# Moving the softmax denominators' small operations in the first two batches, and clearing less of a buffer

## The chip, the cores and the metric

The kernel runs on one core of a Trainium2 chip. The metric is the device time of one execution in microseconds (us), median of several runs. The kernel before takes 1670.19 us (three runs, 1670.05 to 1670.26). Five engines work beside each other, each through its own queue of instructions: TensorE (PE in the profile; PEld is its weight load), VectorE (DVE), ScalarE (ACT), GpSimd (POOL) and SyncE (SP), which issues most of the DMA transfers. All arithmetic is in fp32.

## The reference

Eight batches of eight heads, 576 positions, 64 values per head. Attention drops scores more than `tau` below the row's maximum; a Fourier mixing and a two-layer network follow:

```
scores = (q @ k.T) / 8
scores = where(scores >= max(scores) - tau, scores, -1e9)
attn   = exp(scores - max(scores))
attn   = attn / (sum(attn) + 1e-9)
x      = attn @ v                      # heads side by side: (8, 576, 512)
u      = x + real(fft(fft(x, axis=1), axis=2))
un     = (u - mean(u)) / sqrt(var(u) + 1e-6)
out    = u + relu(un @ w_ch1) @ w_ch2
```

The change concerns `sum(attn) + 1e-9`, its inverse, and where the inverse meets the product with `v`.

## The kernel before

**Steps.** Heads are taken in pairs, four pairs to a batch. A pair has five steps: four of 128 query rows of both heads, and one (`t == 4`) of the last 64 rows of both heads in one tile. So a batch has 20 steps (`per_batch`), numbered `i` over all batches.

**Softmax of a step** (`softmax`, from L450). TensorE puts the scores of the two heads in two PSUM tiles `sc` (L433; L444 in the fifth step). VectorE takes the negated maxima (L461), ScalarE the exponentials `e` (L469) and the threshold `thr` (L473). VectorE then masks `e` and sums it into `den` in one instruction per head (L477), adds 1e-9 (L482, one per head) and takes the reciprocal of both (L489). The scores' tiles are free for the next step when both L477 are done.

**Two ways to divide.** From the third batch on (`normalized`), VectorE and ScalarE multiply `e` by the reciprocal (L492, L496). In the first two batches GpSimd instead spreads the reciprocals over 64 columns per head (`rec`, L501); TensorE transposes this next to the weights, ScalarE copies it to `recs`, and VectorE multiplies by `recs` as it takes the product with `v` out of PSUM (L597).

**Transposed weights of a step** (`weights_in_parts`, L512, called whole by `transposed_weights`). It follows one step behind: after the softmax of step `i` has been issued, step `i - 1` is transposed. TensorE transposes the last 64 keys of both heads (`e[:, 512:640]`, L541) and `rec` (L544) into the tile `pe`, then the other keys (L560) into `pw`. ScalarE copies `pe` to `ends` and `recs` (L548, L552), and `pw` to `e_t` (L562, L564). `weighted_values` (L569) multiplies `v` with `e_t` and lastly `ends` (`pv`, L589).

**Beside it in the first two batches** the network's weights come in. They arrive as 64-bit floats and are converted in chunks of 128x512 (`convert`, L281) by every engine in turn: VectorE takes mantissa and exponent bits (L298, L301), ScalarE turns them into floats (L306, L309, L312), VectorE adds the low word (L314), and GpSimd multiplies by exponent and sign (L319, L320). The first batch converts 16 chunks of `w_ch1`, one in a step. The second batch converts 16 chunks of `w_ch2` by a table (`PLAN`, L1271), in some steps two, while TensorE already runs the Fourier mixing and the network's first groups (L822, L848).

**Order.** Up to the end of the second batch the order on every engine is the program's order (`by_hand`, closed at L1384). In `step` (first batch) and `second_batch` it is: scores, softmax of step `i` with the last stages of the previous chunk between maxima and exponentials, the filler or mixing work, the next chunk's first stages, `transposed_weights(i - 1)`, and more work. In the first batch the first stages of a chunk (L298, L301) come ahead of `transposed_weights`; in the second batch they are issued by `transfers`, `advance` and the calls around it, mostly behind it. After the second batch only TensorE's order is fixed by hand, and a planner orders the other engines.

**The folds' buffer.** `f` (L93, four chunks of two halves of `FW` = 304 columns) first holds the rows of a Fourier table for `copy_seq` (L221), and is then cleared whole by GpSimd (L230). Later `fold_rows` (L611) writes folded rows of `x` into it: in each half columns 0 to 142, 143 or 144 in one half, 160, and 161 to 303. The columns in the gap are read by `fold_halves` and by the mixing's matmuls, so they must be zero.

Of the kernel before, what the change touches and what calls it, by code (L numbers as in the profile page):

```python
# [9 lines left out]
FP32 = mybir.dt.float32  # L10
INT32 = mybir.dt.int32
UINT32 = mybir.dt.uint32
ALU = mybir.AluOpType
# [15 lines left out]
def _repeated(ap, n):  # L29

    return bass.AP(
        tensor=ap.tensor,
        offset=ap.offset,
        ap=[list(ap.ap[0]), list(ap.ap[1]), [0, n]],
    )
# [12 lines left out]
def kernel(  # L48
# [12 lines left out]
    nc = tc.nc  # L61
    B, H, S, D = q.shape
# [4 lines left out]
    NT = 5  # L67
# [17 lines left out]
    ps = ctx.enter_context(tc.tile_pool(name="ps", bufs=2, space=bass.MemoryType.PSUM))  # L85
# [7 lines left out]
    f = const.tile([128, ND, 2 * FW], FP32, name="f")  # L93
# [71 lines left out]
    ident = const.tile([128, 128], FP32, name="ident")  # L165
# [5 lines left out]
    for u in range(2):  # L171
# [10 lines left out]
        out=q_scale[:], in0=tau_t[:], scalar1=0.0, scalar2=SCALE, op0=ALU.is_ge, op1=ALU.mult  # L182
# [3 lines left out]
        out=below[:], in0=tau_t[:], scalar1=0.0, scalar2=-3.0e38, op0=ALU.is_lt, op1=ALU.mult  # L186
# [3 lines left out]
        out=tau_pos[:], in0=tau_t[:], scalar1=0.0, scalar2=-1.0, op0=ALU.max, op1=ALU.mult  # L190
# [30 lines left out]
    def copy_seq():  # L221
        nc.gpsimd.memset(seq_xe[:, :, :], 0.0)
        nc.gpsimd.memset(seq_xo[:, :, :], 0.0)
        for u, (pieces, dst, parity, parts) in enumerate(SEQ):
            for p, n in parts:
                for c in range(2):
                    nc.gpsimd.tensor_copy(
                        dst[p : p + n, c, :], f[p : p + n, u, KH * c + parity : KH * (c + 1) : 2]
                    )
        nc.gpsimd.memset(f[:, :, :], 0.0)  # L230

# [145 lines left out]

    heads = {}  # L380
    steps = {}
    xs = {}
    sums = {}

# [33 lines left out]
    def normalized(n):  # L418


        return n >= 2 * NPAIR
# [28 lines left out]
    def softmax(i, between=None, meanwhile=None):  # L450

        t = i % NT
        sc, nh = steps[i]
        neg = sb.tile([128, 2], FP32, tag="neg", bufs=3, name="neg")
        thr = sb.tile([128, 2], FP32, tag="thr", bufs=3, name="thr")
        den = sb.tile([128, 2], FP32, tag="den", bufs=3, name="den")


        e = sb.tile([128, 2 * S], FP32, tag="e", name="e")
        for j in range(nh):  # L460
            nc.vector.tensor_reduce(  # L461
                out=neg[:, j : j + 1], in_=sc[j][:, :, 0:HALF], axis=AXIS_XY, op=ALU.max,
                negate=True,
            )
        if meanwhile is not None:
            meanwhile()
        for j in range(nh):
            ej = e[:, S * j : S * (j + 1)].rearrange("p (c n) -> p c n", c=2)
            nc.scalar.activation(  # L469
                out=ej, in_=sc[j][:, :, 0:HALF], func=ACT.Exp, bias=neg[:, j : j + 1], scale=1.0  # L470
            )
            if j == 0:
                nc.scalar.activation(  # L473
                    out=thr[:, 0:nh], in_=neg[:, 0:nh], func=ACT.Identity,
                    bias=thr_off[:, :], scale=-1.0,
                )
            nc.vector.scalar_tensor_tensor(  # L477
                out=ej, in0=sc[j][:, :, 0:HALF], scalar=thr[:, j : j + 1], in1=ej,
                op0=ALU.is_ge, op1=ALU.mult, accum_out=den[:, j : j + 1],
            )  # L480

            nc.vector.tensor_scalar(  # L482
                out=den[:, j : j + 1], in0=den[:, j : j + 1], scalar1=1e-9, scalar2=None,
                op0=ALU.add,
            )
            if between is not None:
                between()
                between = None
        nc.vector.reciprocal(den[:, 0:nh], den[:, 0:nh])  # L489
        rec = None  # L490
        if normalized(i // NT):
            nc.vector.tensor_scalar(  # L492
                out=e[:, 0:S], in0=e[:, 0:S], scalar1=den[:, 0:1], scalar2=None, op0=ALU.mult
            )
            if nh == 2:
                nc.scalar.activation(  # L496
                    out=e[:, S : 2 * S], in_=e[:, S : 2 * S], func=ACT.Copy, scale=den[:, 1:2]
                )
        else:
            rec = sb.tile([128, 2 * D], FP32, tag="rec", name="rec")  # L500
            nc.gpsimd.tensor_copy(  # L501
                rec[:, :].rearrange("p (j d) -> p j d", j=nh), _repeated(den[:, 0:nh], 2 * D // nh)
            )
        if t == 4:
            nc.scalar.copy(e[:, S : S + 64], e[:, 512:S])
        steps[i] = (e, rec)

    def transposed_weights(i):
        for _ in weights_in_parts(i):
            pass  # L510

    def weights_in_parts(i):  # L512

        n, t = divmod(i, NT)
        e, rec = steps.pop(i)
        if t in (0, 2):

            e_t = sb.tile([128, 8, S - 256], FP32, tag="e_t", bufs=1, name="e_t")  # L520
            ends = sb.tile([128, S - 256], FP32, tag="ends", bufs=1, name="ends")
            recs = None
            if rec is not None:
                recs = sb.tile([128, S - 256], FP32, tag="sums", bufs=1, name="recs")
            vt = heads[n][2]
            if t == 0 and PAIRS[n % NPAIR] % 2:

                vt = sb.tile([128, 10, D], FP32, tag="vr", bufs=1, name="v_rev")
                src = heads[n][2]
                nc.gpsimd.tensor_copy(vt[:, :, 0:1], src[:, :, 0:1])  # L530
                last = src[:, :, D - 1 : D]
                down = bass.AP(
                    tensor=last.tensor, offset=last.offset,
                    ap=[list(last.ap[0]), list(last.ap[1]), [-1, D - 1]],
                )
                nc.gpsimd.tensor_copy(vt[:, :, 1:D], down)
            heads[n] = (*heads[n][0:2], vt, e_t, ends, recs)
        e_t, ends, recs = heads[n][3:6]
        q0 = 128 * (t - (0 if t < 2 else 2))
        pe = ps.tile([128, 4, 128], FP32, tag="mm", bufs=4, name="pe")  # L540
        nc.tensor.transpose(pe[:, 0, :], e[:, 512:640], ident[:, :])  # L541
        kept = [ends]
        if rec is not None:
            nc.tensor.transpose(pe[:, 1, :], rec[:, :], ident[:, :])  # L544
            kept.append(recs)
        for c, dst in enumerate(kept):
            if t < 4:
                nc.scalar.copy(dst[:, q0 : q0 + 128], pe[:, c, :])  # L548
            else:
                for j in range(2):  # L550
                    hp = slice(64 * j, 64 * j + 64)
                    nc.scalar.copy(dst[hp, q0 : q0 + 64], pe[hp, c, hp])  # L552
        qs = slice(q0, q0 + (128 if t < 4 else 64))
        for j in range(2 if t < 4 else 1):
            pw = ps.tile([128, 4, 128], FP32, tag="mm", bufs=4, name="pw")
            if j == 1:
                yield
            for c in range(4):
                c0 = (S + D) * j + 128 * c
                nc.tensor.transpose(pw[:, c, :], e[:, c0 : c0 + 128], ident[:, :])  # L560
            if t < 4:
                nc.scalar.copy(e_t[:, 4 * j : 4 * j + 4, qs], pw[:, :, :])  # L562
            else:
                nc.scalar.copy(  # L564
                    e_t[:, :, qs].rearrange("p (j c) q -> p j c q", j=2),
                    pw[:, :, :].rearrange("p c (j q) -> p j c q", j=2),
                )

    def weighted_values(n, part):  # L569

# [614 lines left out]
    def step(i):  # L1185
# [9 lines left out]
        if t == 1 and n > 0:  # L1195
            softmax(i, lambda: weighted_values(n - 1, 1), last_stages)
            load_v(n + 1)
        elif t == 3:
            softmax(i, lambda: weighted_values(n, 0), last_stages)
        else:  # L1200
            softmax(i, None, last_stages)
# [56 lines left out]
    load_v(1)  # L1258
    copy_dim(raw)
    copy_seq()  # L1260
    LAST = HID // WC - 1
    for g in range(LAST):
# [124 lines left out]
    for i in range(2 * per_batch, total + 1):  # L1387
# [4 lines left out]
        n, t = divmod(i, NT)  # L1392
        if t > 2:
            fold_more()
        nothing = iter(())
        prep = prep_in_parts(n + 1) if t == 3 and n + 1 < B * NPAIR else nothing
        weights = weights_in_parts(i - 1)
        next(prep, None)
        fill()
# [71 lines left out]
```

## Time and profile before

| engine | busy, us | share of the span | instructions |
|---|---|---|---|
| TensorE (PE) | 1621.8 | 97% | 10826 |
| VectorE (DVE) | 1146.0 | 69% | 2518 |
| ScalarE (ACT) | 837.9 | 50% | 1817 |
| GpSimd (POOL) | 581.9 | 35% | 779 |

The span of the profiled execution is 1669.6 us. The first two batches' steps fill the time up to about 290 us. The instructions of which the change speaks, with their durations over the whole run:

| line | engine, operation | count | median, ns |
|---|---|---|---|
| L482 | DVE, add 1e-9, 128x1 | 288 | 153 |
| L489 | DVE, reciprocal, 128x2 or 128x1 | 160 | 166 |
| L477 | DVE, mask and sum, 128x576 | 288 | 810 |
| L501 | POOL, copy to `rec`, 128x128 | 40 | 438 |
| L230 | POOL, memset of `f`, 128x2432 | 1 | 2292 |
| L298 / L301 | DVE, bits of a chunk, 128x512 | 32 / 32 | 568 and 642 in the two larger groups / 510 and 513 |
| L319 / L320 | POOL, two multiplications of a chunk | 32 / 32 | 1273 / 1293 in the larger groups |

A line of the timeline gives the start in us from the beginning of the span, the duration in us, the engine, the line, the operation, the output and inputs by the program's names, and in brackets how long the engine had been idle and what ended that.

### The profile page before, as it was taken

How to read it: one execution, taken by the hardware profiler on the slowest of the kernel's cores; microseconds unless marked ns; L12 is line 12 of the kernel's file. 1: busy time of each engine (PE TensorE's matmuls, PEld its weight loads, DVE VectorE, ACT ScalarE, POOL GpSimd, SP SyncE). 2: the span in 40 equal slices, each digit the busy share in tenths (PEclk: the TensorE clock that was granted, in tenths of full speed). 3: DMA queues.
4: the chain of work that ended last, by engine and by line, in shares of the span. 5: the costliest groups of instructions: out<-in, count | busy, mean ns of one | idle time of the engine just before them, and what ended most of it. 6: DMA issues, size and time to landing. Idle time of an engine off the chain costs nothing.

```text
span 1669.6 us, 28885 instructions
## 1 busy us (share of the span) xinstructions
PE 1621.8 (97%) x10826; PEld 1273.6 (76%) x10826; DVE 1146.0 (69%) x2518; ACT 837.9 (50%) x1817; POOL 581.9 (35%) x779
## 2 busy tenths in 40 slices
PE   8998899999999999999999999999999999999998
PEld 4555555577887888878888778887878788889998
DVE  6887785567757686857566858686677768664454
ACT  5775675544455454545354546454646455532111
POOL 5674562041321442134332143213242244215232
PEclk9999999999999999999999999999999999999999
DMA  5423222100010101000101010111001010000000
GB/s 157 121 55 110 73 73 56 30 20 21 19 39 15 29 15 42 23 28 8 28 22 35 10 34 15 42 22 29 22 16 42 22 32 4 14 1 13 14 13 13
DMA packets 130384, 57.48 MB, mean 34 GB/s; under 512 B 121123, under 2 KB 121125, under 8 KB 130246
## 3 DMA queue, kind: packets, MB, share of 16 engines
q1 hardware_dynamic: 128854, 55.35, 12.3%
q8 instruction: 86, 1.41, 0.4%
q14 instruction: 52, 0.43, 0.1%
q10 hardware_dynamic: 1392, 0.30, 0.1%
HBM read 46.02 MB, written 9.44 MB: 33 GB/s over the span
## 4 chain that ended last, share of the span: by engine, by line
PE 76%; DVE 15%; ACT 7%; issue 2%; POOL 1%; DVEq 0%; ACTq 0%; POOLq 0%
PE ph L926 23%; PE po L1090 18%; PE pv L589 8%; PE sc L433 7%; PE pw L560 5%; PE po L848 3%; DVE e L477 3%; DVE neg L461 2%; ACT e L469 2%; DVE hs L1051 2%; PE sc L444 2%; PE ph L822 1%; PE py L692 1%; PE pa L709 1%; PE pn L782 1%
## 5 line engine op out<-in xcount | busy, mean ns | idle before, releaser
L469 ACT ACTIVATE e<-sc,neg 128x576 f32<-128x576 f32 x288 | 212.6, 738 | 238.1 <-DVE neg L461 237.4
L461 DVE TENSOR_REDUCE neg<-sc 128x1 f32<-128x576 f32 x288 | 206.2, 750 | 171.4 <-PE sc L433 158.5
L477 DVE SCALAR_TENSOR_TENSOR e<-sc,thr,e 128x576 f32<-128x576 f32 x288 | 229.7, 811 | 57.5 <-ACT thr L473 54.2
L1090 PE MATMUL po<-w,hs 128*128 128x256 f32 x1024 | 246.3, 383 | 0.5 <-DVE u L804 0.5
L1090 PEld LDWEIGHTS po<-w,hs 128*128 128x128 f32 x1024 | 186.0, 190 | 33.6 <-issue 11.2
L926 PE MATMUL ph<-u_t,w 128*128 128x128 f32 x1536 | 187.2, 276 | 0.0
L926 PEld LDWEIGHTS ph<-u_t,w 128*128 128x128 f32 x1536 | 178.7, 192 | 4.4 <-issue 3.3
L560 PE MATMUL pw<-ident,e 128*128 128x128 f32 x1152 | 169.5, 274 | 10.4 <-ACT kT L406 2.7
L562 ACT COPY e_t<-pw 128x512 f32<-128x512 f32 x256 | 148.9, 596 | 59.8 <-PE pw L560 59.3
L433 PE MATMUL sc<-kT,qT 64*128 64x288 f32 x1024 | 168.6, 429 | 6.8 <-DVE e L477 6.0
L560 PEld LDWEIGHTS pw<-ident,e 128*128 128x128 f32 x1152 | 134.2, 141 | 29.3 <-issue 4.3
L935 DVE TENSOR_TENSOR hs<-ph,hs 128x512 f32<-128x512 f32 x160 | 106.9, 685 | 71.4 <-PE ph L926 46.8
L433 PEld LDWEIGHTS sc<-kT,qT 64*128 64x128 f32 x1024 | 93.2, 186 | 69.3 <-issue 37.2
L926 PE MATMUL ph<-t_u,s_w 128*128 128x128 f32 x1024 | 126.0, 276 | 2.2 <-POOL t_u L900 1.8
L804 DVE SCALAR_TENSOR_TENSOR u<-po,rstd,u 128x256 f32<-128x256 f32 (+1 forms) x164 | 75.4, 484 | 73.8 <-PE po L1090 71.9
L926 PEld LDWEIGHTS ph<-t_u,s_w 128*128 128x128 f32 x1024 | 119.4, 192 | 5.3 <-issue 2.6
L1090 PE MATMUL po<-hs,s_tile 128*128 128x256 f32 x512 | 122.1, 382 | 0.0
L496 ACT ACTIVATE e<-e,den 128x576 f32<-128x576 f32 x96 | 75.0, 781 | 67.4 <-DVE den L489 66.7
L1090 PEld LDWEIGHTS po<-hs,s_tile 128*128 128x128 f32 x512 | 93.6, 190 | 13.6 <-issue 2.1
L943 ACT ACTIVATE hs<-hs 128x512 f32<-128x512 f32 x112 | 69.4, 631 | 63.9 <-DVE hs L935 63.9
L622 POOL TENSOR_TENSOR half<-x 128x287 f32<-128x287 f32 x48 | 40.4, 862 | 125.5 <-ACT x L595 70.7
L1086 POOL TENSOR_TENSOR hs<-hs,s_tile 128x512 f32<-128x512 f32 x32 | 42.3, 1323 | 117.5 <-PE po L1090 113.8
(199 smaller groups left out, 2905.8 us busy)
## 6 DMA issues: line engine op xcount, KB each, us to landing
hs<-in_moe_w_ch_dram SPq DMA_DIRECT2D x23, 512.0 KB, 4.4
out_dram<-u SPq DMA_DIRECT2D x36, 256.0 KB, 2.2
qk_in<-in_q_dram SPq DMA_DIRECT2D x64, 128.0 KB, 2.3
v_in<-in_v_dram SPq DMA_DIRECT2D x64, 128.0 KB, 2.4
qk_in<-in_k_dram SPq DMA_DIRECT2D x31, 128.0 KB, 2.5
w<-in_moe_w_ch_dram SPq DMA_DIRECT2D x6, 512.0 KB, 8.4
qk_in<-in_k_dram SPq DMA_DIRECT2D x31, 64.0 KB, 2.3
stage<-in_moe_w_ch_dram SPq DMA_DIRECT2D x3, 512.0 KB, 3.8
```

The lines of the kernel that those rows point to most:

```text
L433: nc.tensor.matmul(sc[j][:, c, 0:HALF], qT[hp, 128 * t : 128 * t + 128], kT[hp, HALF * c : HALF * (c + 1)], start=True, stop=True,)
L461: nc.vector.tensor_reduce(out=neg[:, j : j + 1], in_=sc[j][:, :, 0:HALF], axis=AXIS_XY, op=ALU.max, negate=True,)
L469: nc.scalar.activation(out=ej, in_=sc[j][:, :, 0:HALF], func=ACT.Exp, bias=neg[:, j : j + 1], scale=1.0)
L477: nc.vector.scalar_tensor_tensor(out=ej, in0=sc[j][:, :, 0:HALF], scalar=thr[:, j : j + 1], in1=ej, op0=ALU.is_ge, op1=ALU.mult, accum_out ...
L496: nc.scalar.activation(out=e[:, S : 2 * S], in_=e[:, S : 2 * S], func=ACT.Copy, scale=den[:, 1:2])
L560: nc.tensor.transpose(pw[:, c, :], e[:, c0 : c0 + 128], ident[:, :])
L562: nc.scalar.copy(e_t[:, 4 * j : 4 * j + 4, qs], pw[:, :, :])
L589: nc.tensor.matmul(pv[64 * j : 64 * j + 64, 0:m], vt[:, 2 * c + j, :], e_t[:, 4 * j + c, 0:m] if c < 4 else ends[:, 0:m], start=(c == 0), ...
L804: nc.vector.scalar_tensor_tensor(out=u, in0=product, scalar=self.rstd[:, t : t + 1], in1=u, op0=ALU.mult, op1=ALU.add,)
L926: nc.tensor.matmul(banks[name][:, 128 * q : 128 * q + 128], left[c][:, 512 * part + 128 * q : 512 * part + 128 * q + 128], right[c], start ...
L935: nc.vector.tensor_tensor(out=to, in0=bank, in1=to if other is None else other, op=ALU.add)
L1090: nc.tensor.matmul(bank[:, 0 : DM // 2], left[p], right[p], start=start and p == 0, stop=p == NK - 1, skip_group_check=True,)
```

## The change

In the first two batches the 1e-9 leaves VectorE: one GpSimd instruction for both heads follows the softmax. The reciprocal (VectorE) and the copy to `rec` (GpSimd) become a closure in a list, `inverses`, which is emptied behind the next step's maxima, and also at the head of `weights_in_parts`. There the transposes of `e[:, 512:640]` and `rec` go behind the others. The aim is that VectorE has fewer small instructions between the masking and the work that follows. The clearing of `f` shrinks to the columns from 143 to 159 of each half, so that GpSimd is done sooner in the first step. The batches from the third on keep their form.

```diff
-        nc.gpsimd.memset(f[:, :, :], 0.0)
+        halves = f[:, :, :].rearrange("p d (c n) -> p d c n", c=2)
+        nc.gpsimd.memset(halves[:, :, :, S // 4 - 1 : 160], 0.0)
...
+        while inverses:
+            inverses.pop(0)()
         if meanwhile is not None:
             meanwhile()
...
-            nc.vector.tensor_scalar(
-                out=den[:, j : j + 1], in0=den[:, j : j + 1], scalar1=1e-9, scalar2=None,
-                op0=ALU.add,
-            )
+            if normalized(i // NT):
+                nc.vector.tensor_scalar(
+                    out=den[:, j : j + 1], in0=den[:, j : j + 1], scalar1=1e-9, scalar2=None,
+                    op0=ALU.add,
+                )
...
-        nc.vector.reciprocal(den[:, 0:nh], den[:, 0:nh])
         rec = None
         if normalized(i // NT):
+            nc.vector.reciprocal(den[:, 0:nh], den[:, 0:nh])
...
         else:
             rec = sb.tile([128, 2 * D], FP32, tag="rec", name="rec")
-            nc.gpsimd.tensor_copy(
-                rec[:, :].rearrange("p (j d) -> p j d", j=nh), _repeated(den[:, 0:nh], 2 * D // nh)
-            )
+            nc.gpsimd.tensor_scalar(
+                out=den[:, 0:nh], in0=den[:, 0:nh], scalar1=1e-9, scalar2=None, op0=ALU.add
+            )
+            def inverse():
+                nc.vector.reciprocal(den[:, 0:nh], den[:, 0:nh])
+                nc.gpsimd.tensor_copy(
+                    rec[:, :].rearrange("p (j d) -> p j d", j=nh),
+                    _repeated(den[:, 0:nh], 2 * D // nh),
+                )
+            inverses.append(inverse)
...
     def weights_in_parts(i):
+        while inverses:
+            inverses.pop(0)()
...
-        pe = ps.tile([128, 4, 128], FP32, tag="mm", bufs=4, name="pe")
-        nc.tensor.transpose(pe[:, 0, :], e[:, 512:640], ident[:, :])
...
+        def last_keys():
+            pe = ps.tile([128, 4, 128], FP32, tag="mm", bufs=4, name="pe")
+            nc.tensor.transpose(pe[:, 0, :], e[:, 512:640], ident[:, :])
...
+        if rec is None:
+            last_keys()
         qs = slice(q0, q0 + (128 if t < 4 else 64))
...
+        if rec is not None:
+            last_keys()
```

More of the change, by code (lines that the diff above doesn't have):

```diff
@@ L381 @@
     steps = {}
+    inverses = []
     xs = {}
@@ L539, in weights_in_parts @@
         q0 = 128 * (t - (0 if t < 2 else 2))
-        pe = ps.tile([128, 4, 128], FP32, tag="mm", bufs=4, name="pe")
-        nc.tensor.transpose(pe[:, 0, :], e[:, 512:640], ident[:, :])
[L542 to L552, printed above, removed]
+        def last_keys():
+            pe = ps.tile([128, 4, 128], FP32, tag="mm", bufs=4, name="pe")
+            nc.tensor.transpose(pe[:, 0, :], e[:, 512:640], ident[:, :])
+            kept = [ends]
+            if rec is not None:
+                nc.tensor.transpose(pe[:, 1, :], rec[:, :], ident[:, :])
+                kept.append(recs)
+            for c, dst in enumerate(kept):
+                if t < 4:
+                    nc.scalar.copy(dst[:, q0 : q0 + 128], pe[:, c, :])
+                else:
+                    for j in range(2):
+                        hp = slice(64 * j, 64 * j + 64)
+                        nc.scalar.copy(dst[hp, q0 : q0 + 64], pe[hp, c, hp])
+        if rec is None:
+            last_keys()
         qs = slice(q0, q0 + (128 if t < 4 else 64))
@@ L567, in weights_in_parts @@
                 )
+        if rec is not None:
+            last_keys()
     def weighted_values(n, part):
```

## The prediction

> **What bounds the kernel now.** I read the page first. TensorE is busy 97% of the span, yet the change lives only in the first two batches, so I asked for busy time by stretch.
>
> ```profile
> 0.00:100.00 100.00, 92.61 (x452) 51.36 (x453) 78.24 (x191) 67.81 (x147) 64.64 (x116) 0.98 0.46 130
> 100.00:200.00 100.00, 88.86 (x507) 55.04 (x506) 77.82 (x173) 60.83 (x145) 52.76 (x62) 0.98 0.27 77
> 200.00:300.00 100.00, 93.90 (x505) 56.12 (x504) 71.70 (x174) 62.06 (x143) 45.93 (x63) 0.98 0.24 66
> 300.00:400.00 100.00, 99.01 (x564) 63.79 (x563) 63.74 (x146) 48.71 (x108) 18.77 (x29) 1.00 0.10 26
> ```
>
> (Columns: stretch and length, then busy PE, PEld, DVE, ACT, POOL.) From 264 us on the chain of waits is nearly all TensorE. Before that it alternates between VectorE, ScalarE and TensorE. So what the first 264 us win or lose arrives whole at the end; nothing later can absorb it. Next, the timeline of VectorE and GpSimd in the first step and in one step of batch 1 (the second batch):
>
> ```profile
> 16.40 0.15 DVE L482 TENSOR_SCALAR den<-den 128x1 f32<-128x1 f32 x1
> 16.58 0.17 DVE L489 RECIPROCAL den<-den 128x2 f32<-128x2 f32 x1
> ...
> 16.86 2.29 POOL L230 MEMSET f<- 128x2432 f32 x1
> 17.01 2.42 DVE L301 TENSOR_SCALAR hs<-hs 128x512 int32<-128x512 int32 x1
> ...
> 25.09 0.20 POOL L530 COPY v_rev<-v_in 128x10 f32<-128x10 f32 x1 [0.52 <-DMA v_in<-in_v_dram]
> ...
> 71.00 0.42 DVE L298 TENSOR_SCALAR w<-hs 128x512 int32<-128x512 int32 x1
> ```
>
> ```profile
> 192.97 1.58 POOL L319 TENSOR_TENSOR w<-w,u_t 128x512 f32<-128x512 f32 x1 [7.33 <-DVE w L314]
> 194.63 1.29 POOL L320 TENSOR_TENSOR w<-w,w 128x512 f32<-128x512 f32 x1
> 195.88 1.46 POOL L319 TENSOR_TENSOR w<-w,u_t 128x512 f32<-128x512 f32 x1
> 197.42 1.36 POOL L320 TENSOR_TENSOR w<-w,w 128x512 f32<-128x512 f32 x1
> 198.73 0.29 POOL L501 COPY rec<-den 128x128 f32<-128x128 f32 x1
> ```
>
> ```profile
> 195.31 0.17 DVE L489 RECIPROCAL den<-den 128x2 f32<-128x2 f32 x1
> 195.39 0.81 DVE L298 TENSOR_SCALAR w<-w 128x512 int32<-128x512 int32 x1
> 196.13 1.50 DVE L301 TENSOR_SCALAR u_t<-w 128x512 int32<-128x512 int32 x1
> 197.55 1.41 DVE L461 TENSOR_REDUCE neg<-sc 128x1 f32<-128x576 f32 x2
> ```
>
> Two things are to be seen. L298 and L301 take 0.42 us alone and up to 1.5 us (2.42 under the memset) while GpSimd works. And in the step at 193 us GpSimd still multiplies weights until 198.8, 3.7 us after the last masking (L477) ended at 195.1.
>
> [...]L301 and the memset end within 0.3 us of each other, while the maxima L461 take 736 to 767 ns everywhere. [...]each engine's rows follow its program order. So a reciprocal that waits for GpSimd holds everything behind it on VectorE.
>
> **The change, part by part.**
>
> *Where the inverse goes.* The pending inverses are emitted behind the next maxima, but also at the head of the function that transposes weights. That function is called for step i-1 just after the softmax of step i has queued its inverse, so step i's reciprocal is emitted there. The order of the built instructions shows it: in batch 0 behind L298 and L301 of its own step, ahead of the next maxima; in batch 1 mostly straight behind L477, ahead of L298 and L301. Only steps 0 and 19 fall behind maxima. GpSimd's 1e-9 stands behind the L319/L320 pairs of that step.
>
> *Memset.* 2432 elements in a partition become 136. At 2.29 us for the whole I take 0.25 (the 288-element memset took 0.35; bounds 0.15 and 0.35). L301 then ends near 17.4 instead of 19.4, 1.9 us earlier. But L530 waits for a DMA until 25.09, and L319 stands behind it, so GpSimd's pair gains only some 1.0 us by then. I count **-1.0** (bounds -1.9 and -0.5).
>
> *Additions off VectorE (72 of them, 40 steps of two or one).* L482 lasts 153 ns. The chain before holds 25 pieces of it (3.9 us) and 11 of L489 (1.7 us). Most of this isn't won, for two reasons. In batch 0 a conversion step is a loop: L314 ends, 0.14, the two multiplies 2.65, L298 ends 0.25 after them, L301 0.43, maxima 1.33, L314 0.67: 5.47 us, against 5.42 and 5.43 between L314 at 20.7, 26.1 and 31.5. [...]In the other steps only the second L477 moves, by 0.11 us (its start after the first one's end). The page of waits gives 16 score matmuls waiting for L477; at about 8 of them the 0.11 counts: **-0.9**.
>
> *Reciprocal in batch 0.* It takes 0.17 us behind L301, but the copy to rec (0.28 to 0.57) no longer slows L301 (0.51 instead of 0.42). Even: **0**. The copy to rec now waits about 1 us more on GpSimd. That is hidden where GpSimd idles 1 to 4 us before L319, but not between 95.9 and 110.7, where it never idles (L377, the folds L627, L651, L652, and the pairs). Two such waits cost 0.4 to 0.8[...]: **+1.0**.
>
> *Addition on GpSimd.* No row shows it. A 128x2 operation there (L632) takes 0.20; I take 0.25 with 0.1 for each handover, bounds 0.15 and 0.5. Where GpSimd is idle that equals the two removed instructions. Where it is busy, VectorE waits for the last L320. Batch 1, from the old times:
>
> - 176-180: GpSimd free at 179.0[...], reciprocal 179.4, L301 ends 180.4 instead of 179.6: +0.8. ScalarE's L309 and the next exp wait for it.
> - 184: L320 to 184.7, L298 ends 185.4 instead of 184.95, part given back: +0.3.
> - 193-199: four multiplies end at 198.4, reciprocal 198.8, L298 and L301 end near 200.5[...] instead of 197.6. The next maxima, exp, the copies of e_t behind exp on ScalarE, then pv and the next scores on TensorE wait: +2.9.
> - 207-210: +0.4. 213-220, four multiplies again, but the old L298/L301 were already held to 220.3: +0.8.
> - 236: L320 to 236.9, then L622 beside L298/L301: they end about 238.9 instead of 237.6: +1.2. TensorE's ph at 239.46 waits for ScalarE behind it.
> - 160, 168, 222-229, 242, 249: 0. Hidden behind L728 to L735, TensorE's ph and pv, and waits for pv of 1.2 to 1.5 us.
>
> Sum **+6.4**.
>
> *Last keys after the other transposes.* ScalarE then copies e_t before ends and recs. At 225.0 and 259.7 those copies (0.85 us) stood between the exp and e_t, for which pv waits: **-1.7**. Elsewhere ScalarE's total is the same and the order costs nothing, since rec leaves slack (in one step it was ready at 48.0 us and transposed at 50.9).
>
> Together: -1.0 - 0.9 + 1.0 + 6.4 - 1.7 = +3.8 us on 1670.2: **1674.0**. Batches 2 to 7 keep their instructions and order.
>
> **The rivals.**
> - *The removed work pays in full*: 3.9 + 1.7 + 1.9 = 7.5 us, 1662.7; with half of it 1666.4. For it: all those pieces are on the chain. Against it: [...]an inverse that isn't behind the maxima.
> - *TensorE hides both sides*: it is 94% busy from 200 to 300 us, and pv at 226.5 took 3.8 us for what takes 2.4 elsewhere, so there is slack. Then only the memset's 1.0 and some of the 1.7 stay against 1 to 3 of stalls: about 1670.5.
> - *The stalls add up*: 3.9 at 193, 1.6 at 236, 1.0 at 176 and 213, 1.5 at 95-110, no gain from additions: +8, 1678.
>
> **How the numbers follow.** Forecast 0.55, full pay 0.15, hidden 0.18, stalls add up 0.12. The forecast spreads about 2 us either way and 3.3 us (0.2%) is the bound, so a third of it falls within no change. Slower: 0.37 + 0.12 = 0.49; same: 0.18 + 0.18 = 0.36; faster 0.15. The range leaves out the better half of full pay and the far end of the worst case: 1667.0 to 1679.0.
>
> **What would show it.** Right: in the profile after, the reciprocal has idle time before it released by GpSimd's addition, some 3 us of it in the step near 193 us; L301 of the first step near 0.45 us; maxima of the third step about 1 us earlier. Compare the start of batch 2's first maxima (289.7 before): I expect about 293.5. Wrong: no idle time before the reciprocal, or a stall at 193 us after which the scores that stood at 204.4 have not moved.

## The result and the profile after

The changed kernel takes **1680.8 us** (median of four runs, 1680.04 to 1681.69) against 1670.21 for the kernel before: ratio 1.0064, 95% interval 1.0046 to 1.0081, so 10.6 us (0.6%) slower. The forecast was 1674.0 with a range up to 1679. The direction was right, the size was not.

Busy time by stretch, as before (length, then PE, PEld, DVE, ACT, POOL, granted clock, DMA share, GB/s):

```profile
0.00:100.00 100.00, 92.39 (x476) 52.71 (x478) 81.52 (x169) 69.51 (x153) 68.31 (x133) 1.00 0.47 131
100.00:200.00 100.00, 87.37 (x482) 53.42 (x478) 67.34 (x143) 55.77 (x134) 51.51 (x72) 0.97 0.26 77
200.00:300.00 100.00, 89.94 (x463) 53.02 (x462) 62.30 (x137) 62.14 (x142) 49.24 (x77) 0.93 0.22 61
```

In the second and third stretch VectorE is about 10 us less busy than before and TensorE does less as well (463 matmul records instead of 505 from 200 to 300). TensorE's granted clock has fallen there, from 0.98 to 0.97 and 0.93; in the first stretch it has risen from 0.98 to 1.00.

The first step (lines have moved: L300, L303 are the old L298, L301; L232 the clearing, L507 GpSimd's addition, L512 the reciprocal, L513 the copy to `rec`):

```profile
15.59 0.54 DVE L303 TENSOR_SCALAR hs<-hs 128x512 int32<-128x512 int32 x1
...
17.23 0.22 POOL L232 MEMSET f<- 128x136 f32 x1
...
17.53 0.23 POOL L507 TENSOR_SCALAR den<-den 128x2 f32<-128x2 f32 x1
...
17.79 0.17 DVE L512 RECIPROCAL den<-den 128x2 f32<-128x2 f32 x1 [0.28 <-POOL den L507]
```

L303 takes 0.54 us instead of 2.42, and the clearing 0.22 instead of 2.29. (That the first follows from the second is not so, as the second experiment below shows.) Already here VectorE idles 0.28 us until GpSimd has added 1e-9. What VectorE waited for in the first 305 us (total, times, longest):

```profile
DVE den L512 <- POOL den L507: 27.1, 22, 3.9
DVE e L482 <- ACT thr L478: 17.0, 26, 1.5
```

The first line did not exist before. Its longest wait is in the step that the prediction named:

```profile
197.56 1.29 POOL L322 TENSOR_TENSOR w<-w,w 128x512 f32<-128x512 f32 x1
...
198.93 0.21 POOL L507 TENSOR_SCALAR den<-den 128x2 f32<-128x2 f32 x1
199.18 0.17 DVE L512 RECIPROCAL den<-den 128x2 f32<-128x2 f32 x1 [3.94 <-POOL den L507]
...
199.26 1.04 DVE L300 TENSOR_SCALAR w<-w 128x512 int32<-128x512 int32 x1
200.22 1.01 DVE L303 TENSOR_SCALAR u_t<-w 128x512 int32<-128x512 int32 x1
200.33 0.63 ACT L308 ACTIVATE w<-w 128x512 f32<-128x512 int32 x1 [5.49 <-DVE w L300]
...
201.16 1.41 DVE L464 TENSOR_REDUCE neg<-sc 128x1 f32<-128x576 f32 x2
...
202.97 0.48 PE L561 MATMUL pe<-ident,e 128*128 128x128 f32 x1 [2.73 <-ACT hs L852]
...
204.98 4.07 PE L614 MATMUL pv<-e_t,v_rev 128*64 128x256 f32 x16 [1.32 <-ACT e_t L585]
```

GpSimd's addition of 0.21 us stands behind the multiplications of a chunk that end at 198.9. VectorE idles 3.94 us, and L300, L303 and the next maxima behind its reciprocal with it. ScalarE, whose L308 needs L300, idles 5.49 us, and its copy of the network's `ph` out of PSUM (L852, from 202.44) stands behind L308 to L314. TensorE waits 2.73 us for that copy, and then 1.32 us for `e_t`, which ScalarE copies behind the exponentials. The windows after two such steps (columns as above):

```profile
115.00:120.00 5.00, 5.00 (x14) 2.85 (x14) 3.25 (x7) 1.79 (x4) 2.43 (x5) 0.50 0.00 0
...
200.00:205.00 5.00, 0.95 (x6) 0.34 (x4) 4.40 (x8) 4.36 (x9) 3.79 (x7) 0.80 0.41 134
205.00:210.00 5.00, 5.00 (x22) 2.55 (x24) 2.24 (x6) 2.56 (x6) 3.89 (x9) 0.52 0.02 3
```

From 200 to 205 us TensorE works 0.95 us of 5. In the next 5 us it is full, but at a granted clock of 0.52 and with 22 matmul records. The kernel before has 31 there:

```profile
205.00:210.00 5.00, 5.00 (x31) 3.49 (x28) 4.23 (x12) 4.42 (x13) 4.01 (x8) 1.00 0.00 0
```

In the record of the clock in these two traces it is either 1.00 or 0.50 (half clock). In the first 300 us it is at 0.50 from 114.2 to 121.1, 203.0 to 209.8, 233.7 to 237.1 and 247.3 to 250.8 us in the changed kernel, 20.5 us in all, and from 17.9 to 21.3, 110.1 to 113.5 and 226.1 to 229.5 us, 10.2 us in all, in the profile of the kernel before. A window's 0.52, 0.66 or 0.73 is a mean over both. That stalls would be followed by such stretches was not in the prediction.

### The profile page after: what moved, and what is told of

The parts are those of the page before. It is cut to its first block, busy times and chain, and to the rows that moved or that the text cites. A ratio compares the mean times of both kernels' runs of the same rounds, so it can differ in the third digit from the quotient of the medians.

```text
span 1679.3 us, 28816 instructions
## 1 busy us (share of the span) xinstructions
PE 1626.3 (97%) x10826; PEld 1276.2 (76%) x10826; DVE 1135.3 (68%) x2446; ACT 836.8 (50%) x1817; POOL 587.4 (35%) x819
## 4 chain that ended last, share of the span: by engine, by line
PE 74%; DVE 14%; ACT 5%; POOL 3%; issue 2%; DMA 1%; SPq 1%; ACTq 0%; POOLq 0%; DVEq 0%
PE ph L951 23%; PE po L1115 18%; PE pv L614 8%; PE sc L436 6%; PE pw L583 5%; PE po L873 3%; DVE neg L464 2%; DVE hs L1076 2%; DVE e L482 2%; PE sc L447 2%; ACT e L474 2%; PE ph L847 2%; PE py L717 1%; POOL w L321 1%; PE pa L734 1%
## 5 line engine op out<-in xcount | busy, mean ns | idle before, releaser
L482 DVE SCALAR_TENSOR_TENSOR e<-sc,thr,e 128x576 f32<-128x576 f32 x288 | 228.2, 813 | 55.0 <-ACT thr L478 51.4
L583 PEld LDWEIGHTS pw<-ident,e 128*128 128x128 f32 x1152 | 135.6, 142 | 41.2 <-issue 14.6
```

The source lines that it names most:

```text
L482: nc.vector.scalar_tensor_tensor(out=ej, in0=sc[j][:, :, 0:HALF], scalar=thr[:, j : j + 1], in1=ej, op0=ALU.is_ge, op1=ALU.mult, accum_out ...
```

## The experiments

The place where time goes can be read from the start of each step's first masking. The lag is this start less that of the same step in the kernel before. The table gives the change of the lag over a stretch (us). These are single profiles: beside a noise of some tenths, a stretch at half clock in only one of the two moves a row by some 1.5 us. Row 30 to 31 has one in the kernel before (226.1 to 229.5 us), so 1.45 us of each gain there are no merit of the variant. The table is used throughout:

| steps (start in the kernel before) | changed | addition not waited for | no addition, inverse as changed | no additions, inverse as before |
|---|---|---|---|---|
| 0 to 15 (14.6) | -2.13 | -1.39 | -1.62 | -2.56 |
| 15 to 20 (106.7) | +3.11 | -0.01 | -0.63 | -0.37 |
| 20 to 26 (136.3) | +0.38 | -0.39 | -0.47 | -0.27 |
| 26 to 28 (193.3) | +5.07 | +1.59 | -0.22 | -0.31 |
| 28 to 30 (207.6) | +1.49 | -0.95 | -0.87 | -0.84 |
| 30 to 31 (224.2) | -0.70 | -2.45 | -2.55 | -2.55 |
| 31 to 33 (234.0) | +3.25 | +3.98 | +5.34 | -0.03 |
| 33 to 40 (247.8) | -0.90 | -0.77 | -0.77 | -0.76 |
| together | +9.57 | -0.39 | -1.79 | -7.69 |

From step 40 (third batch) on the lag of the changed kernel stays at its value, but for one place: 1.6 us more come between steps 62 and 63, with a stretch at half clock (534.1 to 537.5 us) that the profile of the kernel before does not have. The first masking itself comes 1.0 us sooner than in the kernel before. The two spans differ by 9.7 us, the medians by 10.6.

Four things compete: VectorE's wait for GpSimd's addition, the inverse's new place, GpSimd's 40 further instructions (the expectations say 36; the trace has 40 rows of L507), and what the clearing and the order of the last keys do. Medians of different experiments are compared by their ratios to the kernel before, times 1670.

### The small parts alone

The clearing alone, in the kernel before:

```diff
-        nc.gpsimd.memset(f[:, :, :], 0.0)
+        nc.gpsimd.memset(halves[:, :, :, S // 4 - 1 : 160], 0.0)
```

> The kernel before with the smaller memset alone. If the 2 us that L301 loses under the memset carry to the end: 1668 us. If the wait for the DMA of a later chunk (1.9 us before L298 of the third step in the changed kernel) or of v takes them back: 1669.5 to 1670.3 us.

Measured: 1669.33 us, ratio 0.9996 (0.9987 to 1.0004), no gain clear of the noise. In the profile (of an execution of 1667.59 us, one of the two fastest of twelve) the lag changes by -1.71 us up to step 1, and +1.22 comes back between steps 2 and 3, where VectorE waits for the third chunk's transfer:

```profile
27.31 0.90 DVE L300 TENSOR_SCALAR w<-hs 128x512 int32<-128x512 int32 x1 [0.95 <-DMA hs<-in_moe_w_ch_dram]
```

In the changed kernel the same line waits 1.90 us. So much of the sooner first step is given to a transfer. And the sooner first step is not shown to be the clearing's work: the next experiment still clears the whole buffer, and its lag changes by -1.84 us up to step 1.

The order of the last keys alone, in the kernel before (`pe` is transposed and copied behind `pw`):

```diff
+        if rec is not None:
+            last_keys()
```

> The kernel before with the transposes of the last keys and of rec behind the others in the first two batches, nothing else. Theory A: it does little or gains the 1.7 us that e_t waits behind ends and recs: 1668 to 1670.5 us. Rival B (this order is what costs): above 1674 us.

Measured: 1667.63 us, ratio 0.9988 (0.9981 to 0.9995), 2.0 us faster. In its first step the whole clearing starts behind L301 and doesn't disturb it:

```profile
16.75 0.54 DVE L301 TENSOR_SCALAR hs<-hs 128x512 int32<-128x512 int32 x1
...
17.52 2.13 POOL L230 MEMSET f<- 128x2432 f32 x1
```

In the profile of the kernel before it started 0.15 us ahead of L301. So the 2.42 us of L301 there come from an overlap that need not arise with the whole clearing in place; besides, TensorE's clock was at 0.50 there from 17.9 to 21.3 us.

The lag changes by -2.32 between steps 30 and 31 and by -0.88 between 35 and 36. Of the first, 1.45 is TensorE's clock: from 225 to 230 us it was 0.66 before and is 1.00 here, and the clearing alone also has 1.00 there and gains 1.45. The other 0.87 is the order: `e_t` no longer stands behind `ends` and `recs` on ScalarE, and TensorE's gap ahead of `pv` is 0.9 us shorter. The kernel before, the clearing alone, and the last keys' order alone:

```profile
226.53 3.83 PE L589 MATMUL pv<-e_t,v_rev 128*64 128x320 f32 x16 [2.51 <-ACT e_t L564]
...
224.21 2.37 PE L591 MATMUL pv<-e_t,v_rev 128*64 128x320 f32 x16 [2.52 <-ACT e_t L566]
...
224.56 2.37 PE L595 MATMUL pv<-e_t,v_rev 128*64 128x320 f32 x16 [1.62 <-ACT e_t L568]
```

The first two have the same gap of 2.5 us, and only in the first of them do the matmuls behind it take 3.83 us, at half clock.

Both together:

> The kernel before with the smaller memset and the last keys' transposes behind the others: the change without its inverses and its addition on GpSimd. Their gains add if they lie at different places (0.5 and 2.2 us alone): 1666.5 to 1667.5 us, faster than before and than the changed kernel.

Measured: 1667.67 us, ratio 0.9989 (0.998 to 0.9997). They don't explain a loss; they hide about 1.8 us of it. The clearing adds nothing here to the last keys' order (0.9988 alone).

### The inverse's place and the additions' engine

All of the change, but with the two 128x1 additions on VectorE again, behind each masking:

```diff
-            nc.gpsimd.tensor_scalar(out=den[:, 0:nh], ..., scalar1=1e-9, scalar2=None, op0=ALU.add)
+            nc.vector.tensor_scalar(out=den[:, j : j + 1], ..., scalar1=1e-9, scalar2=None, op0=ALU.add)
```

> The changed kernel with the two 128x1 additions of 1e-9 back on VectorE behind each masking, as before; memset, order of transposes and place of the inverse as changed. It differs from e2 only in the addition's form (128x2 in e2, which took up to 1.3 us under GpSimd's multiplications, 128x1 here, which never took over 0.16 us). What is left of the cost is the copy of rec, which now stands behind the fold's two subtractions on GpSimd (in e2 TensorE waited 3.3 us for it at 240 us and its clock fell). Theory A with that second wait: 1669.5 to 1672.5 us. If the addition on GpSimd was the only cost: 1666 to 1668 us.

Measured: 1668.7 us, ratio 1.0000 (0.9991 to 1.0008). The whole loss is gone once the additions are back on VectorE.

The addition back on VectorE as one 128x2 instruction, directly ahead of the reciprocal:

```diff
             def inverse():
+                nc.vector.tensor_scalar(out=den[:, 0:nh], in0=den[:, 0:nh], scalar1=1e-9, ...)
                 nc.vector.reciprocal(den[:, 0:nh], den[:, 0:nh])
```

> The changed kernel, but the 1e-9 is added by VectorE again, one instruction for both heads directly ahead of the reciprocal, at the place the changed kernel gives the reciprocal. No wait for GpSimd is left; everything else (memset, order of transposes, place of the inverse) is as changed. Theory A: 1666 to 1671 us, the slips from step 26 on gone. Rival B: above 1677 us. Rival C (GpSimd's load): some 3 us less than the changed kernel.

Measured: 1673.33 us, ratio 1.0024 (1.0017 to 1.0032). That is 4 us slower than with two instructions of half the width. VectorE's groups of this kernel show why (busy us, mean ns, idle before):

```profile
L508 DVE TENSOR_SCALAR den<-den 128x2 f32<-128x2 f32 x32 | 14.9, 467 | 0.5
L508 DVE TENSOR_SCALAR den<-den 128x1 f32<-128x1 f32 x8 | 1.2, 145 | 0.1
```

The 128x2 form takes 467 ns in the mean and up to 1308 ns: 18 of the 32 took 0.15 to 0.17 us, 14 took 0.38 to 1.31. Each of those above 300 ns began beside a GpSimd instruction on two tensors and ended within 0.05 us of the end of one. Three of the eight 128x1 additions at the same place began beside such an instruction too, and took 136 to 153 ns; in the kernel before 74 of them took 154 in the mean. So the long times came with the form, not with the place. In sum the longer form costs VectorE about 5 us (14.9 less an estimated 9.9 for 64 additions of 154 ns). TensorE's wait for `rec` near 240 us, of which more below, is no difference between the two kernels: its longest piece is 3.3 us in both. But in this kernel's profile the clock stands at 0.50 for 17.1 us of the first 300, and in that of the two instructions for 3.4. How the 4 us divide is open.

The inverse really behind the next step's maxima (the head of `weights_in_parts` empties only inverses of its own step and older ones):

```diff
-        while inverses:
+        while inverses and inverses[0].step <= i:
```

> The changed kernel, but the head of weights_in_parts takes only the inverses of its own step or earlier ones, so that each reciprocal stands behind the maxima of the next step as the change in words says. Theory A (the reciprocal waits on VectorE for GpSimd's addition, which queues behind the L319/L320 multiplications; 27.1 us of such idle time in the changed kernel): that idle time falls below 6 us, the +3.2, +1.1 and +1.6 us slips between steps 26 and 33 go, and the time is 1664 to 1671 us. Rival B (the transposes in another order, or the DMA of the third chunk, cost it): the time stays above 1677 us. Rival C (GpSimd itself is longer by the additions): 1675 to 1679 us.

Measured: 1674.12 us, ratio 1.0027 (1.0017 to 1.0037). VectorE's wait for GpSimd falls to 0.7 us, as hoped, and a new one takes its place on TensorE:

```profile
PE pe L565 <- POOL rec L513: 17.6, 13, 2.6
```

`rec` is now too late for its transpose, 13 times. So the later place takes away 6.2 of 10.7 us; the 4.5 that are left stand beside 17.6 us of new waits on TensorE.

The opposite, the inverse emitted straight behind GpSimd's addition:

```diff
-            inverses.append(inverse)
+            inverse()
```

> The changed kernel, but the inverse is emitted at once, behind the addition on GpSimd, ahead of everything else of the step. Theory A: VectorE now waits for GpSimd in the first batch too, ahead of L298 and L301, and idles some 45 us or more in front of the reciprocal instead of 27; the copy to rec is back ahead of the folds. 1682 to 1692 us. If the order of the copy to rec and the folds on GpSimd were the main cost, it would come down to 1675 us or less.

Measured: 1689.47 us, ratio 1.0119 (1.0102 to 1.0135). VectorE's wait doubles, and the loss nearly does (19.9 us):

```profile
DVE den L512 <- POOL den L507: 53.1, 40, 3.9
```

### No addition at all, and one that nobody waits for

The kernel with the small clearing and the last keys' order, the inverse as before, and no addition in the first two batches (a sum there is at least 1, since the row's maximum contributes exp(0), and 1e-9 is below what its fp32 form resolves):

```diff
-            nc.vector.tensor_scalar(out=den[:, j : j + 1], ..., scalar1=1e-9, scalar2=None, op0=ALU.add)
+            if normalized(i // NT):
+                nc.vector.tensor_scalar(out=den[:, j : j + 1], ..., scalar1=1e-9, scalar2=None, op0=ALU.add)
```

> e8 (the kernel before with the smaller memset and the last keys' transposes behind the others) with the 1e-9 left out in the first two batches: 72 additions of 0.15 us fewer on VectorE, nobody waits for them, nothing takes their place. This bounds what taking them off VectorE could bring. If the chain's 3.9 us of additions were all to be won: 1663.5 to 1665 us. [...]

Measured: **1663.45 us**, ratio 0.9968 (0.9955 to 0.998). It beats both kernels. Against the same kernel with additions (0.9989) it is 3.5 us faster (the intervals meet at 0.998), close to the 3.9 us that the chain of the kernel before held in L482. By the forecast's 0.9 us for the additions it would have been 1666.8 us.

The changed kernel with GpSimd's addition left out:

```diff
-            nc.gpsimd.tensor_scalar(out=den[:, 0:nh], in0=den[:, 0:nh], scalar1=1e-9, ...)
```

> The changed kernel with GpSimd's addition left out: 1e-9 is not added in the first two batches, where a sum is at least 1 and 1e-9 is below what its fp32 form resolves. The inverse is copied, taken and applied at the changed kernel's place, behind the next step's maxima; the order of the last keys and the small clearing stay as changed. Theory A (VectorE's wait for GpSimd's addition is what costs): nothing is waited for, so the time is that of the kernel without additions, 1663.5, plus the about 1 us that the inverse's new place cost when both additions stood on VectorE: 1664 to 1666. Rival B (the inverse's new place costs): 1670 or more.

Measured: 1668.23 us, ratio 0.9994 (0.9986 to 1.0003). This falls between the two expectations. It differs from the kernel just above in the inverse's place alone, and is 4.3 us slower (intervals apart). The table puts most of the difference in one place, steps 31 to 33 (5.4 of 5.9 us). Its timeline there:

```profile
232.72 1.54 POOL L643 TENSOR_TENSOR half<-x 128x287 f32<-128x287 f32 x2 [3.19 <-DMA x<-swap]
...
234.21 0.29 POOL L509 COPY rec<-den 128x128 f32<-128x128 f32 x1
...
234.55 0.47 PE L560 MATMUL pe<-ident,rec 128*128 128x128 f32 x1 [3.73 <-POOL rec L509]
```

and that of the kernel with the inverse at the old place:

```profile
229.91 0.49 POOL L504 COPY rec<-den 128x128 f32<-128x128 f32 x1
...
231.11 0.27 PE L548 MATMUL pe<-ident,rec 128*128 128x128 f32 x1
```

The inverse is emitted one call later, and by then a fold (L643), which waits 3.19 us for a transfer, has been issued to GpSimd. The copy to `rec` stands behind it, TensorE waits 3.73 us for the copy, and its granted clock in the following 235 to 240 us is 0.50. So the new place has a cost of its own, apart from the addition. How large it is depends on the clock too: with the additions back on VectorE, TensorE had a gap of 3.3 us at the same copy (from 232.9 us), its clock stayed at 1.00, and the place cost 1.8 us (1.0000 less 0.9989, intervals overlapping).

The changed kernel with GpSimd's addition made, but into a tile that nobody reads:

```diff
-                out=den[:, 0:nh], in0=den[:, 0:nh], scalar1=1e-9, ...
+                out=spare[:, 0:nh], in0=den[:, 0:nh], scalar1=1e-9, ...
...
-                nc.vector.reciprocal(den[:, 0:nh], den[:, 0:nh])
+                nc.vector.reciprocal(inv[:, 0:nh], den[:, 0:nh])
...
-                    _repeated(den[:, 0:nh], 2 * D // nh),
+                    _repeated(inv[:, 0:nh], 2 * D // nh),
```

> The changed kernel with GpSimd's addition still made, on the same sums and in the same place of its queue, but into a tile that nobody reads; the reciprocal reads the sums themselves, so 1e-9 does not reach the output in the first two batches. GpSimd's load is that of the changed kernel, VectorE's wait for it is gone. Theory A (the wait costs): within 1.5 us of the kernel without GpSimd's addition, 1664 to 1667. Rival C (GpSimd's 36 further instructions cost[...]): 1672 or more. In between, both have a share, and the difference to the kernel without the addition is C's.

Measured: 1670.85 us, ratio 1.0005 (0.9996 to 1.0013), again between the two. Against the changed kernel only VectorE's wait is missing, and 9.9 us are gone (1.0064 less 1.0005; the intervals are well apart). Against the kernel without GpSimd's addition, GpSimd's 40 instructions cost 1.8 us by the medians, but those intervals overlap, so this share isn't settled. In the table it lies at steps 26 to 28, where the copy to `rec` also comes late and the clock is at 0.50 from 199.8 to 203.2 us.

### TensorE's clock after the gaps

The changed kernel with six matmuls on `ones` put into `pw` ahead of the transposes of steps 26 and 31 (the transposes overwrite them), so that TensorE doesn't stand idle:

```diff
+            if j == 0 and i in (26, 31):
+                for _ in range(6):
+                    nc.tensor.matmul(pw[:, :, :], ones[:, :], four, start=True, stop=True)
```

> The changed kernel with six 128x512 filler matmuls ahead of the transposes of steps 26 and 31, written into a tile that the transposes then overwrite[...]. If the gap itself costs, nothing changes: 1680 to 1681 us. If the gaps also lower TensorE's clock afterwards (0.52 in 205 to 210 us, where 20 matmuls of pv took 4.9 us instead of 2.6; eight of ph 4.54 instead of 2.85 at 247 us), the clock stays at 1.00 there, the slips after steps 27 and 32 shrink by 1.5 to 2 us each, and the time is 1676.5 to 1678 us.

Measured: 1679.78 us, ratio 1.0059 (1.0044 to 1.0074): inconclusive as a time. Six fillers took 5.3 us, twice the author's estimate, so the second group overran its gap. The lag shows both: +0.47 instead of +1.89 between steps 27 and 28, +3.12 instead of +1.68 between 32 and 33. With three fillers at steps 15, 26 and 31:

> The changed kernel with three 128x512 filler matmuls (0.87 us each, as e5 showed) ahead of the transposes of steps 15, 26 and 31, so that they end inside the gaps in front of the scores at 113.6, of pv at 205.0 and of ph at 247.2 us of the changed kernel's trace. VectorE's waits stay as they are. If TensorE's clock after a gap is part of the cost: the clock stays near 1.00 at these places, each slip shrinks by 1 to 2 us, 1676 to 1678.5 us. If the waits alone cost: 1680 to 1681 us.

Measured: 1676.9 us, ratio 1.0045 (1.0031 to 1.0059). The same windows as above in this kernel:

```profile
115.00:120.00 5.00, 4.42 (x24) 2.73 (x23) 3.21 (x8) 2.89 (x7) 2.58 (x6) 1.00 0.00 0
...
205.00:210.00 5.00, 5.00 (x34) 3.26 (x31) 3.60 (x7) 3.23 (x6) 2.42 (x7) 1.00 0.00 0
```

The clock is 1.00, and from 205 to 210 us 34 matmul records fit where 22 did. VectorE's wait for the addition is unchanged (27.2 us, 22 times). By ratios the clock is worth 3.2 us of the 10.7, by the lag at step 40 of single profiles 6.3 (+3.29 instead of +9.57). The ratios' intervals overlap. The sign is shown by the windows, and by the mean clock of every execution: 0.996 to 0.999 in five with three fillers, 0.992 to 0.994 in four of the changed kernel. The size stays open between 3 and 6 us; of the 6.3, 1.0 lies at steps 30 to 31, where no filler stands. The fillers don't take the gaps away entirely: 2.5 us without work are left at 201.8 us, and the clock stays at 1.00.

## Why the prediction was off, point by point

- **The mechanism: right.** The reciprocal idles for GpSimd's addition (27.1 us in all, up to 3.94), VectorE's queue stands behind it, and the end moves. Taking the wait away and nothing else takes 9.9 us away.
- **Addition on GpSimd, +6.4, and the stretch from 95 to 110 us, +1.0: most places right, the terms too small. Here the prediction failed.** The six steps with a forecast cost show, on the lag: 176 us +0.67 (forecast 0.8), 184 +0.39 (0.3), 193 +3.18 (2.9), 207 +0.39 (0.4), 213 +1.10 (0.8), 236 +1.57 (1.2). Together 7.3 for 6.4. What failed first is that the working stopped at the stall: it let TensorE go on at the pace of before. After the gap at 193 another 1.89 us went between steps 27 and 28, and 1.68 between 32 and 33, at a reduced clock (0.52 from 205 to 210 us, 0.73 from 245 to 250). With three fillers and the clock at 1.00 these two were 0.31 and 0.54. Second, the waits at 222 to 229 us were put at 0, as hidden. There VectorE waits 3.20 us (at 226.1), TensorE's gap ahead of `pv` is 2.7 us, and row 30 to 31 loses 1.75 against the kernel where nobody waits (-0.70 and -2.45). Third, in the 95 to 110 us stretch the prediction counted a later copy to `rec`, +1.0; steps 15 to 18 lost 3.7. There VectorE waited for the addition itself, 1.49 us at 109.4 and 1.24 at 115.8, and the clock was at 0.50 from 114.2 to 121.1; with three fillers these steps lost 1.6.
- **The reading of 226.5 us as slack: wrong, and the clue was in the profile.** A `pv` of 3.8 us for what takes 2.4 elsewhere was taken by one rival for room on TensorE. It was TensorE at half clock (0.66 as the mean of 225 to 230 us). Read rightly, it would have told what a gap can cost.
- **Additions off VectorE, -0.9: too small.** That most of their 3.9 us would be hidden was the author's estimate, from the loop of a conversion step (5.47 us by its parts). With nobody waiting, leaving them out gave 3.5.
- **Reciprocal in the first batch, 0, and its copy later: incomplete.** Where the copy to `rec` falls behind was checked against L319 and L320, not against a fold that waits for a transfer. In the kernels without a wait, this one place cost 4.3 us. In the changed kernel, whose steps have shifted by then, TensorE waits only 1.3 us for `rec` near 245 us.
- **Clearing, -1.0: not confirmed.** Measured -0.7 (from 2.2 faster to 0.7 slower), and nothing on top of the last keys' order. The 1.9 us read off L301 were an overlap in that profile: with the whole clearing still in place L301 took 0.54 us in the profile of the last keys' order alone. What limits a sooner first step is the third chunk's transfer (VectorE waits 0.95 us for it with the clearing alone, 1.90 in the changed kernel), not the transfer for which L530 waits.
- **Last keys, -1.7: right in size and cause.** Measured -2.0 alone. On the lag the order gave 0.87 at 225 us (2.32 less the clock's 1.45) and 0.88 at 259 us, where the forecast had 0.85 each.
- **What it would show.** Idle of the reciprocal: yes, 27.1 us. L301 of the first step near 0.45: 0.54. Stall of 3 us near 193: 3.94. Maxima of the third step about 1 us earlier: 2.8 (22.0 for 24.8), of which 1.0 is there before the first masking. First maxima of the third batch at 293.5: 298.3. The misses are those named above: the clock, the waits taken as hidden, and the first batch.

By parts, in us: without additions and with the old place -5.3; the inverse's new place +4.3; GpSimd's work +1.8, not settled; VectorE's wait +9.9; sum +10.7. The prediction had gains of 3.6 and costs of 7.4, where the runs show gains of 5.3 and costs of 16.0. The parts are differences in this order and need not be the same in another: with the additions on VectorE the new place cost 1.8. The clock's share lies inside these parts, not beside them.

## What to carry to other kernels

A small instruction moved to a less busy engine costs its place in that engine's queue (here a wait of up to 3.94 us), not its 0.2 us: ask what stands ahead of it there, and what stands behind the one that waits for it. When a stall reaches TensorE, reckon with slow microseconds after the gap beside the gap: here 1.89 us more went behind the gap at 203 us, and 0.31 where the clock stayed at 1.00. A duration that one profile shows can be a chance overlap: look for it in a second profile before counting on it. And before moving an operation, ask whether it is needed: here leaving it out gave the largest gain of all versions.

## What was not expected of the hardware

- **TensorE's clock after short gaps.** In the changed kernel the granted clock fell to 0.50 at 114.2 us, behind 2.3 us without work (111.3 to 113.6), and at 203.0 us, at the end of 2.7 us without work. The length of a gap alone does not decide: behind 2.5 us ahead of `pv` the clock was 0.50 in the kernel before and 1.00 with the clearing alone, and behind 3.3 us (from 232.9) it was 1.00 with the additions back on VectorE. What decides is not shown here.
- **Two-element additions on VectorE beside GpSimd's work.** With GpSimd at work beside them, 128x2 additions took up to 1308 ns, while the 74 additions of 128x1 in the kernel before stayed within 150 and 155 ns, 56 of them begun while GpSimd worked. What sets the two forms apart is not shown here. In this kernel two one-element instructions (about 0.31 us) were cheaper than one of two elements (0.467 us in the mean).
